# A convolution in two channel passes, merged with a gated layer by a planner that writes the order of every instruction

## The chip, the cores and the metric

The kernel runs on one core of a Trainium2 chip. The metric is the device time of one execution in microseconds; the figure for the kernel before is the median of three runs. Engines are named as the profile names them: PE (TensorE), DVE (VectorE), ACT (ScalarE), POOL (GpSimd), SP (SyncE, which here issues all DMAs).

## What is computed

The input x (2048 positions, 512 channels) goes through two layers, mixed by a gate per position. All is fp32.

```
g  = sigmoid((x * gate_w).sum(-1))
dt = exp(log_dt);  logdA = dt * (A_re + i A_im)                    # 512 x 128
K[d, l] = Re sum_n  C[d,n] * exp(logdA[d,n] * l) * dt * B[d,n]      # l = 0..2047
a  = causal_convolution(x, K, along positions) + x * Dskip          # by FFT in the reference
h  = sigmoid(x @ w_gate) * (x @ w_up)                               # 512 -> 1792
b  = h @ w_down                                                     # 1792 -> 512
out = g * a + (1 - g) * b
```

## The kernel before, in words

**The gated layer** (`glu`, `weights`, `hidden`, L303 to L352 and L373 to L412). Positions are cut into two halves, each into two blocks `sb` of 512. The 1792 hidden columns are 14 tiles `f` of 128, in groups of 4, 4, 3 and 3. Each fp32 operand is split into a high part, rounded to fp32r, and the rest, and a product is three fp32r matmuls (high x high, low x high, high x low). `hidden` makes one tile of h with 24 matmuls (L401), ACT's sigmoid (L408), DVE's product (L409), and the split of h (L410, L411). After each group the down product takes 3 matmuls a tile for each of four blocks of 128 positions (L339), and the result goes to `acc`, by ACT for the first group (L343), by DVE after that (L345). That makes 1344 + 672 matmuls. Weights are loaded and split twice: the first half stores the low part in DRAM (`wlo`), the second loads the raw weights again, rounds them again, and reads the low part back.

**K** (`bases`, `double`, `kgen`, L147 to L241). The 512 channels are 16 groups of 32, with the 128 states n on the partitions. l is written as a sum of two indices, so the exponential is a product of two tables of complex powers, T[:, 0] with 32 entries and T[:, 1:3] with 64. Each is built by doubling: a table of e entries times one power gives the next e, three DVE operations a step (L187, L188, L189: product with the imaginary part, product with the real part, sum). Both tables are doubled together up to 32, and one more step of 128 x 2048 elements makes 64. PE sums over n with 64 products of 32 x 64 a group (L220, `kps`); ACT evicts (L223), DVE adds Dskip, PE applies the first transform step to K (L232), ACT evicts to `kev` (L236), and each two of these tiles of four groups go to DRAM (`a_k`).

**The convolution.** `rows` (L354) takes 16 blocks of x, makes the gate, transforms (L367, two products that use 64 rows of the array each) and stores to `a_u`. When all K is there, `finish` (L252) goes through 16 steps q over all 512 channels: the second step of the transform for x and K (L248, 128 rows by 64 columns, two column halves side by side), the complex product on DVE (L268 to L275), three copies on ACT (L276 to L278) that stack real and imaginary parts in 128 rows, the inverse step (L281), and a store to `b_s`. `final` (L287) reads `b_s` back for each block of 128 positions, applies the last step (L293) and adds g times it to `acc` (L296).

**What sets the order.** The body is written as Python generators. `run_b` lets the gated layer go on by a number of matmuls (`ROW`, `MID`, `END`, `LAST`, L44) at fixed points of the other work. The layer that records the program then sets the order in which the instructions of each engine stand; the last part of `kgen` has high priority. Each engine works through its own stream in order. All DMAs are issued by SP.

Of the kernel before, what the change touches and what calls it, by code (L numbers as in the profile page):

```python
# [13 lines left out]

# [6 lines left out]
F32 = mybir.dt.float32  # L22
# [7 lines left out]
P = 128  # L30
# [4 lines left out]
NG = 16  # L35
KS = [6, 0, 7, 1, 8, 2, 9, 3, 10, 4, 5]
NB = len(KS)
# [3 lines left out]
NQ = 4  # L41

UNITS = 2 * 12 * NF * 6
ROW, MID, END, LAST = 32, 50, 0.7, 0.14  # L44


def constants():
# [5 lines left out]
    wk = np.zeros((4, 32, 2, 4, 32))  # L53
    wf = np.zeros((2, 2, 32, 2, 32))
    for j in range(2):
        for c in range(2):
            for jp in range(2):
                wu[jp, j, :, jp, c, j, :] = fwd[c]
            wf[j, c, :, j, :] = fwd[c].T / L
    for j in range(4):  # L60
        for c in range(2):
            wk[j, :, c, j, :] = fwd[c]
# [3 lines left out]
    for k in range(32):  # L66
# [6 lines left out]
    wv = wv.reshape(16, 2, P, P).transpose(0, 2, 1, 3)  # L73
    e2 = 2.0 ** np.array(KS)
    f = lambda x, *s: np.ascontiguousarray(x.astype(np.float32).reshape(s))
    return {
        "c_wu": f(wu, P, 2, P), "c_wf": f(wf, P, 64), "c_wk": f(wk, P, 2, P),
        "c_pw": f(np.stack([e2, e2 / (2 * np.pi) * np.where(np.array(KS) < 6, -1, 1)]), 1, 2 * NB),
        "c_w2": f(w2, 16, P, 2 * P), "c_wv": f(wv, 16, P, 2 * P),
# [3 lines left out]
def body(ctx, tc, xp, xt, prm, ldt, dsk, gw, wgu, wdn, c_wu, c_wf, c_wk, c_w2, c_wv, c_pw, out):  # L83
    nc = tc.nc
    mm = nc.tensor.matmul
    pool = lambda name, bufs=1, space=None: tc.tile_pool(name=name, bufs=bufs, **({"space": space} if space else {}))

    dr = ctx.enter_context(pool("dr", 1, DRAM))
    a_u = dr.tile([2, 64, 32, D], F32, name="a_u")
    a_k = dr.tile([NQ, P, 32, P], F32, name="a_k")  # L90
    b_s = dr.tile([P, 32, D], F32, name="b_s")
    dts = dr.tile([16, 32], F32, name="dts")
    wlo = dr.tile([NF, P, 1536], F32, name="wlo")
# [3 lines left out]
    bp = ctx.enter_context(pool("bp"))  # L97
    ps = ctx.enter_context(pool("ps", 1, PSUM))

    def fps(tag="fft", bufs=2):  # L100
        return ps.tile([P, 512], F32, tag=tag, bufs=bufs, name="fps")


    wu = cst.tile([P, 2, P], F32, name="wu")
    wk = cst.tile([P, 2, P], F32, name="wk")
    pw = cst.tile([P, 2, NB], F32, name="pw")
    gwb = cst.tile([P, D], F32, name="gwb")
# [5 lines left out]
    nc.vector.memset(hpi, math.pi / 2)  # L113


    def steps():
        st = bp.tile([16, 10, 32], F32, tag="sg", bufs=2, name="steps")
        x, nf, r, e, h1, h2 = (st[:, i] for i in range(6))
        n, pn, b1, b2 = (st[:, i].bitcast(I32) for i in range(6, 10))
        nc.sync.dma_start(x, ldt)  # L120
        V = nc.vector
        V.tensor_scalar(x, x, -104.0, 89.0, op0=OP.max, op1=OP.min)
        V.tensor_scalar(n, x, 1 / math.log(2), None, op0=OP.mult)
        V.tensor_copy(nf, n)
        V.scalar_tensor_tensor(r, nf, -LN2H, x, op0=OP.mult, op1=OP.add)
        V.scalar_tensor_tensor(r, nf, -LN2L, r, op0=OP.mult, op1=OP.add)
        V.tensor_scalar(e, r, 1 / 5040, 1 / 720, op0=OP.mult, op1=OP.add)
        V.tensor_tensor(e, e, r, op=OP.mult)
        for k in (120, 24, 6, 2, 1):
            V.scalar_tensor_tensor(e, e, 1.0 / k, r, op0=OP.add, op1=OP.mult)  # L130
        V.tensor_scalar(e, e, 1.0, None, op0=OP.add)

        for s in (0.5, 1.0):
            V.tensor_scalar(pn, nf, s, None, op0=OP.mult)
            h, b = (h1, b1) if s < 1 else (h2, b2)
            V.tensor_copy(h, pn)
            if s == 1.0:
                V.tensor_tensor(h, h, h1, op=OP.subtract)
# [5 lines left out]
    def tmp(pp):  # L144
        return pp.tile([P, 2048], F32, tag="tmp", bufs=2, name="tmp")
# [359 lines left out]
```

## Time and profile before

| | |
|---|---|
| median of 3 runs | 755.97 us (750.52 to 758.19) |
| the profiled execution: time | 753.36 us |
| the profiled execution: span from the first to the last instruction | 751.6 us |
| mean granted TensorE clock | 0.975 |
| moved by DMA | 118.64 MB, mean 158 GB/s |
| the chain that ended last: PE, DVE, ACT, DMA | 53%, 28%, 8%, 7% |

The page gives busy time of each engine, the span in 40 slices (a digit is a tenth of busy time), the chain of work that ended last, and the costliest groups of instructions by line with count, busy time and mean time of one. PE is the matmuls and PEld the loading of their weights. Matmuls are pipelined, so that a busy PE need not be a PE at its peak: what a matmul costs is read from the time between two starts. A window row gives the busy time of each engine in a stretch of the span.

### The profile page before, as it was taken

To read this page: it belongs to the slowest core of one execution; us is meant where nothing else is said; L and a number is where in the kernel's file an instruction comes from. 1 tells how busy PE (TensorE), PEld (TensorE's weight loads), DVE (VectorE), ACT (ScalarE), POOL (GpSimd) and SP (SyncE) were. 2 spreads that over 40 slices of the span, in tenths; PEclk is the share of its full clock that TensorE was granted. 3 is DMA by queue.
4 is the path that set the end of the run, shared out by engine and by line. 5 is a ranking of instruction groups with operands and counts; after the bars stand their busy time and mean duration, and the time that the engine had idled before them with its cause. 6 is when DMAs were issued, how large, how long until landed. Compare 5 with 4: busy or idle time off the path is not lost.

```text
span 751.6 us, 12658 instructions
## 1 busy us (share of the span) xinstructions
PE 706.8 (94%) x5024; PEld 475.2 (63%) x5024; DVE 604.9 (80%) x835; ACT 375.5 (50%) x611; POOL 3.7 (0%) x36
## 2 busy tenths in 40 slices
PE   4988889998999999999999999999999999999995
PEld 3445348877888778877787787887883323333651
DVE  5888989999999999899999898999944544454343
ACT  5364645763638274655565654546134555555200
POOL 0000000000000000000000000000000000000000
PEclk9789879999999999999999999999999999999999
DMA  6768662433025033565013350531158877774587
GB/s 221 213 204 229 170 178 97 156 104 148 32 88 183 22 115 130 194 237 175 26 57 126 100 189 8 168 115 56 57 187 284 258 241 243 225 223 147 174 285 254
DMA packets 61019, 118.64 MB, mean 158 GB/s; under 512 B 8224, under 2 KB 22944, under 8 KB 59936
## 3 DMA queue, kind: packets, MB, share of 16 engines
q1 hardware_dynamic: 60960, 117.84, 48.3%
q8 instruction: 39, 0.64, 0.3%
q14 instruction: 20, 0.16, 0.1%
HBM read 75.35 MB, written 42.47 MB: 157 GB/s over the span
## 4 chain that ended last, share of the span: by engine, by line
PE 53%; DVE 28%; ACT 8%; DMA 7%; issue 3%; SPq 0%; DVEq 0%; ACTq 0%
PE gups L401 19%; PE dps L339 12%; PE fps L248 9%; DVE T L189 6%; DVE T L188 6%; DVE tmp L187 6%; PE ips L281 4%; PE fps L367 3%; DVE h L409 2%; PE kps L220 2%; DVE hl L411 2%; DMA xs<-xt 2%; PE fps L232 2%; DMA wst<-wgu 1%; PE fps L293 1%
## 5 line engine op out<-in xcount | busy, mean ns | idle before, releaser
L401 PE MATMUL gups<-xh,gu 128*128 128x512 f32 x896 | 293.9, 402 | 15.2 <-ACT gu L381 12.5
L401 PEld LDWEIGHTS gups<-xh,gu 128*128 128x128 f32 x896 | 170.0, 191 | 71.4 <-issue 16.2
L401 PE MATMUL gups<-xl,gu 128*128 128x512 f32 x448 | 179.2, 400 | 0.0
L339 PE MATMUL dps<-dnw,hh 128*128 128x512 f32 x448 | 150.2, 402 | 3.6 <-ACT hh L410 3.0
L187 DVE TENSOR_TENSOR tmp<-T,bz 128x64 f32<-128x64 f32 (+2 forms) x96 | 114.8, 1195 | 2.3 <-issue 0.2
L189 DVE TENSOR_TENSOR T<-T,tmp 128x64 f32<-128x64 f32 (+2 forms) x96 | 114.6, 1194 | 0.7
L188 DVE TENSOR_TENSOR T<-T,bz 128x64 f32<-128x64 f32 (+2 forms) x96 | 114.6, 1193 | 0.0
L339 PEld LDWEIGHTS dps<-dnw,hh 128*128 128x128 f32 x448 | 83.5, 189 | 37.5 <-issue 11.6
L401 PEld LDWEIGHTS gups<-xl,gu 128*128 128x128 f32 x448 | 85.6, 191 | 27.4 <-issue 10.3
L339 PE MATMUL dps<-dnw,hl 128*128 128x512 f32 x224 | 89.6, 401 | 3.0 <-DVE hl L411 1.7
L408 ACT ACTIVATE sg<-gups 128x512 f32<-128x512 f32 x56 | 33.5, 598 | 70.3 <-PE gups L401 69.6
L268 DVE TENSOR_TENSOR t<-fps,uf 128x512 f32<-128x512 f32 x32 | 22.0, 688 | 57.6 <-PE fps L248 47.6
L410 ACT ACTIVATE hh<-h 128x512 fp32r<-128x512 f32 x56 | 35.1, 628 | 47.9 <-DVE h L409 47.9
L409 DVE TENSOR_TENSOR h<-gups,sg 128x512 f32<-128x512 f32 x56 | 38.1, 684 | 20.4 <-PE gups L401 20.1
L339 PEld LDWEIGHTS dps<-dnw,hl 128*128 128x128 f32 x224 | 42.3, 189 | 16.5 <-DVE hl L411 3.7
L411 DVE TENSOR_TENSOR hl<-h,hh 128x512 fp32r<-128x512 f32 x56 | 38.3, 686 | 8.9 <-ACT hh L410 8.4
L381 ACT ACTIVATE gu<-wst 128x1024 fp32r<-128x1024 f32 x28 | 29.6, 1057 | 29.4 <-PE gups L401 13.8
L345 DVE SCALAR_TENSOR_TENSOR acc<-dps,omg,acc 128x512 f32<-128x512 f32 x48 | 35.5, 746 | 10.3 <-PE dps L339 10.3
L248 PE MATMUL fps<-au,w_in 128*64 128x512 f32 x128 | 42.3, 611 | 0.3 <-DVE t L268 0.3
L236 ACT ACTIVATE kev<-fps 128x256 f32<-128x256 f32 x64 | 33.8, 678 | 16.3 <-PE fps L232 15.4
L248 PE MATMUL fps<-ak,w_in 128*64 128x512 f32 x128 | 41.2, 609 | 0.0
L367 PE MATMUL fps<-u,wu 64*128 64x512 f32 x64 | 32.4, 780 | 6.6 <-DMA u<-xp 2.9
(78 smaller groups left out, 664.5 us busy)
## 6 DMA issues: line engine op xcount, KB each, us to landing
wst<-wgu SPq DMA_DIRECT2D x28, 512.0 KB, 4.5
a_u<-evu SPq DMA_DIRECT2D x32, 256.0 KB, 3.3
a_k<-kev SPq DMA_DIRECT2D x8, 1024.0 KB, 6.0
au<-a_u SPq DMA_DIRECT2D x16, 512.0 KB, 4.8
ak<-a_k SPq DMA_DIRECT2D x16, 512.0 KB, 4.2
b_s<-evb SPq DMA_DIRECT2D x32, 256.0 KB, 2.5
b_in<-b_s SPq DMA_DIRECT2D x16, 512.0 KB, 4.6
wsd<-wdn SPq DMA_DIRECT2D x28, 256.0 KB, 3.5
```

The lines of the kernel that those rows point to most:

```text
L187: nc.vector.tensor_tensor(t2, src, sb, op=OP.mult)
L188: nc.vector.tensor_tensor(dst, src, br, op=OP.mult)
L189: nc.vector.tensor_tensor(dst, dst, t2[:, :, ::-1], op=OP.add)
L236: nc.scalar.activation(kv[i][:, s:s + 4], p4[:, :, :, 16 * i:16 * i + 16], AF.Copy)
L248: mm(p[64 * kb:64 * kb + 64], w[:, kb, 64 * c:64 * c + 64], a(kb), start=True, stop=True, tile_position=(0, 64 * kb), skip_group_check=True)
L339: mm(p, a[:, hs], dnw[:, b], start=(n == 0), stop=(n == last))
L345: nc.vector.scalar_tensor_tensor(accs[t], p, omg[:, t:t + 1], accs[t], op0=OP.mult, op1=OP.add)
L367: mm(ph[jp], wu[r, jp], u[r], start=True, stop=True, tile_position=(64 * jp, 0))
L401: mm(p, gu[:, a, k, dc], b[:, dc], start=(n == 0), stop=(n == 11))
L409: nc.vector.tensor_tensor(h, pp[1], sg, op=OP.mult)
L410: nc.scalar.activation(hh, h, AF.Copy)
L411: nc.vector.tensor_tensor(hl, h, hh.bitcast(F32), op=OP.subtract)
```

## The change

The program computes the same, with these differences.

- **The order.** Every piece of work is a generator (a strand) that yields `(engine, cost, function, what it waits for)`. `Plan.run` keeps a clock for each engine, takes the strand whose next piece could start first (its start plus a bias per strand), calls the function, which records the instructions, and books the cost. Costs are constants in the code: `dve(n)` and `act(n)` for n elements, 0.227 a matmul, 1.28 for a change of activation table. `manual_schedule` makes the recorded order the final one. Buffers are single slots, handed out by the planner.
- **K.** The second factor (64 entries) isn't doubled any more. 38 angles per channel and state are formed (`ANGLES`: 0 to 32 and five powers of two), reduced by rounding, and ACT takes sine and cosine of all (L332, L333). ACT also makes 64 magnitudes per channel, with 32 ACTIVATEs of 64 elements a group, each with the scale taken from SBUF (L338). DVE multiplies the two to `B` (L389 to L393), the lower 32 entries with conjugate angles. Only the first factor T (32 entries) is doubled, in five steps (L359 to L361).
- **Packed products.** The first step on K (L434), the inverse step (L582) and the last step (L627) use 64 rows of the array, with the two row halves side by side, and accumulate real and imaginary parts; the three copies that stacked them are gone.
- **Two passes.** The convolution runs over 256 channels at a time (`WIDTHS`). A pass begins when its eight groups of K are stored (`kdone`), so the first pass stands between groups 9 and 12 of K. `a_k` and `b_s` are one DRAM tensor a pass, and a transfer of K to DRAM (L450) has runs of 64 elements.
- **Weights.** The first half stores both parts of the split weights (`wsp`), and the second reads both back; nothing is split twice. Loads and splits go in pieces of 128 x 512.

The gated layer's product is written back to PSUM and split from there. The number of its matmuls, 2016, is the same.

On PE, in the middle of K (the gated layer is L401 and L339 before, L749 and L798 now; kps is the sum over states). Before:

```order
L401 MATMUL gups<-xl,gu 128x512
L220 MATMUL kps<-T 32x64 x64
L339 MATMUL dps<-dnw,hh 128x512
L339 MATMUL dps<-dnw,hl 128x512
L339 MATMUL dps<-dnw,hh 128x512 x2
L339 MATMUL dps<-dnw,hl 128x512
L232 MATMUL fps<-wk,kst 64x128 x16
```

Now, around group 9:

```order
L409 MATMUL kps<-B,T 32x64 x64
L798 MATMUL dps<-dnw,h 128x512 x3
L513 MATMUL s2u<-au,ww 64x256 x4
L749 MATMUL gups<-x,gu 128x512 x6
L513 MATMUL s2u<-au,ww 64x256 x4
L749 MATMUL gups<-x,gu 128x512 x6
L513 MATMUL s2k<-ak,ww 64x256 x4
L798 MATMUL dps<-dnw,h 128x512 x3
L434 MATMUL wps<-wk,kst 64x64 x32
L513 MATMUL s2k<-ak,ww 64x256 x4
L749 MATMUL gups<-x,gu 128x512 x6
L582 MATMUL ips<-y,ww 128x256 x4
```

The first pass of the convolution (L513, L582) has moved between the groups of K, in blocks of four products between three or six matmuls of the gated layer; before, all of it stood behind the last group.

On ACT, the bases of one group (L163 to L172 before, L310 to L346 now; L408/L764 is the sigmoid, L410/L770 the split of h). Before:

```order
L165 ACT_TABLE_LOAD
L165 ACTIVATE tmp<-tmp 128x352
L410 ACTIVATE hh<-h 128x512
L166 ACTIVATE tmp<-tmp 128x352
L167 ACT_TABLE_LOAD
L167 ACTIVATE tmp<-tmp 128x352
L408 ACT_TABLE_LOAD
L408 ACTIVATE sg<-gups 128x512
L382 ACTIVATE dnw<-wsd 128x512
L168 ACT_TABLE_LOAD
L168 ACTIVATE tmp<-tmp,hpi 128x352
L408 ACT_TABLE_LOAD
```

Now:

```order
L331 ACTIVATE mg<-ex 128x1216
L332 ACT_TABLE_LOAD
L332 ACTIVATE ex<-mg,hpi 128x32x38
L770 ACTIVATE h<-gups 128x512
L333 ACTIVATE ex<-ex 128x32x38
L334 ACT_TABLE_LOAD
L334 ACTIVATE e_2473<-e_2473 128x160
L338 ACTIVATE mg<-pw,aa 128x64 x32
L764 ACT_TABLE_LOAD
L764 ACTIVATE sg<-gups 128x512
L346 ACTIVATE bz<-bz 128x160
L770 ACTIVATE h<-gups 128x512
```

The exponentials have become one block of 32 between two table loads, and no sigmoid stands inside it.

On DVE, where the fields of one group are made (B is the second factor, T the first; `mg` are the magnitudes):

```order
L344 TENSOR_TENSOR bz<-ex,e_2834 128x2x160
L376 TENSOR_TENSOR w<-w 128x32
L377 TENSOR_TENSOR w<-w 128x32
L378 TENSOR_TENSOR w<-w,ex 128x64
L379 TENSOR_TENSOR w<-w,ex 128x64
L380 TENSOR_TENSOR T<-w 128x32
L381 TENSOR_TENSOR T<-w 128x32
L425 TENSOR_TENSOR kst<-kst,dskt 128x8
L766 TENSOR_TENSOR gups<-gups,sg 128x512
L389 TENSOR_TENSOR B<-ex,mg 128x64x32
L771 TENSOR_TENSOR h<-gups,h 128x512
L392 TENSOR_TENSOR B<-mg,ex 128x32x32
```

Before, no row of the kind of B existed, and this place held the doubling steps of 128 x 2048 (L187 to L189). A step of the gated layer (L766, which takes a sigmoid `sg`) now stands ahead of B.

The core of the diff:

```diff
+ANGLES = list(range(33)) + [64 << k for k in range(5)]
+NA = len(ANGLES)
+WIDTHS = [256, 256]
...
+    def cost(self, eng, n):
+        if eng == "PE":
+            mode, n = n
+            return n + (0.1 if mode != self.last else 0.0)
+        if eng == "ACT" and isinstance(n, tuple):
+            return n[1] + (1.28 if n[0] != self.kind else 0.0)
+        return n
...
+                    key = start + st[0]
+                    if best is None or key < best[0]:
+                        best = (key, st, eng, m, start)
...
+    ctx.enter_context(tc.manual_schedule())
+    dve = lambda n: 0.067 + n * 1.042e-3
+    act = lambda n: 0.06 + n * 0.88e-3
...
-    def bases(pp, gi):
-        nc.vector.tensor_tensor(th, aa[:, :, None, :].to_broadcast(sh), pw[:, :, :, None].to_broadcast(sh), op=OP.mult)
...
+                V.tensor_tensor(f, aa[:, 1, :, None].to_broadcast([P, 32, NA]), pw[:, None, :NA].to_broadcast([P, 32, NA]), op=OP.mult)
+            t = yield "ACT", act(32 * NA), lambda: A.activation(n, f, AF.Copy), [t, mgs.t]
+            t = yield "DVE", dve(32 * NA), lambda: V.tensor_tensor(f, f, n, op=OP.subtract), [t]
...
+            t = yield "ACT", act(32 * NA), lambda: A.activation(af, f, AF.Abs), [t]
+            t = yield "ACT", ("sin", act(32 * NA)), lambda: A.activation(cs, af, AF.Sin, scale=-2 * math.pi, bias=hpi), [t]
+            t = yield "ACT", ("sin", act(32 * NA)), lambda: A.activation(f, f, AF.Sin, scale=-2 * math.pi), [t]
+            te = yield "ACT", ("exp", act(160)), lambda: A.activation(e5, e5, AF.Exp), [te]
+            def mags():
+                for d in range(32):
+                    A.activation(mg[:, d], pw[:, NA + 5:], AF.Exp, scale=aa[:, 0, d:d + 1])
+            tm = yield "ACT", ("exp", 32 * act(64)), mags, [t]
...
-            double(pp, T[:, 2], T[:, 1], bz, 10, 32, 32)
...
+            yield "DVE", dve(2048), lambda: V.tensor_tensor(
+                B[:, :, :, 32:], ex[:, :, :, :32], mg[:, :, None, 32:].to_broadcast(sh), op=OP.mult), [tb]
+            lo = ex[:, :, :, 32:0:-1]
+            yield "DVE", dve(1024), lambda: V.tensor_tensor(B[:, :, 0, :32], mg[:, :, :32], lo[:, :, 0], op=OP.mult), [tb]
+            tb = yield "DVE", dve(1024) + 0.1, lambda: V.scalar_tensor_tensor(
+                B[:, :, 1, :32], mg[:, :, :32], -1.0, lo[:, :, 1], op0=OP.mult, op1=OP.mult), [tb]
+            for k in range(5):
+                e = 1 << k
+                t = yield from double(T[:, :, :, e:2 * e], T[:, :, :, 0:e], bz[:, :, k], 32, e, t)
...
+            for s in range(8):
+                for jh in range(2):
+                    r = slice(64 * jh, 64 * jh + 64)
+                    for c in range(2):
+                        mm(ph[jh][64 * c:64 * c + 64, 64 * s:64 * s + 64], kst[r, s], wk[r, c], start=True, stop=True,
+                           tile_position=(64 * jh, 64 * c), skip_group_check=True)
...
+            te = yield "SP", kb(1024), lambda: S.dma_start(a_k[j][:, :, o:o + 64], kev), [te]
...
-            nc.scalar.activation(y[:64, 1], y[64:, 0], AF.Copy)
-            nc.scalar.activation(y[64:, 1], t2[64:, 0], AF.Copy)
-            nc.scalar.activation(y[64:, 0], t2[:64, 0], AF.Copy)
-                mm(p, wv[:, kb], y[:, kb], start=True, stop=True)
+            for c in range(2):
+                for i in range(2):
+                    r = slice(64 * i, 64 * i + 64)
+                    mm(pi[i], ww[r, 2 + c], y[r, c], start=(c == 0), stop=(c == 1), tile_position=(64 * i, 0))
...
+            for x in range(4):
+                for jb in range(2):
+                    r = slice(64 * jb, 64 * jb + 64)
+                    mm(ph[jb][32 * x:32 * x + 32], wf[r], b[x // 2][r, x % 2], start=True, stop=True,
+                       tile_position=(64 * jb, 32 * x), skip_group_check=True)
...
+        t1 = yield "SP", kb(1024), lambda: S.dma_start(ga, gf), [t]
+        t2 = yield "SP", kb(512), lambda: S.dma_start(da, df), [t]
+        wstored[f].set(max(t1, t2))
...
+                      (load_x(), 0.0), (load_w(), 0.0), (const("wu", wu, c_wu, kb(128)), 0.2),
+                      (const("gwb", gwb, gw.to_broadcast([P, D]), kb(256)), 0.2), (bases(), 0.2), (tables(), 0.5),
+                      (rows(), 0.0), (const("wk", wk, c_wk, kb(64)), 0.3),
+                      (const("dsk", dskt, dsk.rearrange("p (g s) -> p g s", g=NG), kb(64)), 0.3),
+                      (const("wf", wf, c_wf, kb(16)), 0.4), (hidden(), 1.0), (down(), 0.7), (passes(), 0.1)):
```

898 lines of the change are left out of this document (584 added, 314 removed).

## The prediction

> **What bounds the kernel now.** I read the page's busy line and its 40 slices first, then the table of windows, cut where the last group of K is finished.
>
> ```profile
> PE 706.8 (94%) x5024; PEld 475.2 (63%) x5024; DVE 604.9 (80%) x835; ACT 375.5 (50%) x611; POOL 3.7 (0%) x36
> PE   4988889998999999999999999999999999999995
> DVE  5888989999999999899999898999944544454343
> PEclk9789879999999999999999999999999999999999
> 0.00:20.00 20.00, 9.51 (x28) 6.31 (x28) 11.80 (x44) 10.93 (x16) 0.42 (x6) 1.00 0.70 231
> 20.00:115.00 95.00, 80.89 (x514) 45.36 (x516) 84.27 (x132) 45.91 (x99) 0.43 (x4) 0.82 0.68 194
> 20.00:540.00 520.00, 495.19 (x4156) 380.82 (x4157) 494.18 (x645) 281.86 (x459) 3.24 (x30) 0.97 0.40 128
> 540.00:751.00 211.00, 202.06 (x842) 88.05 (x840) 98.89 (x148) 82.74 (x137) 0.00 (x0) 0.99 0.68 225
> ```
>
> In the window rows the numbers behind the length are busy us (and instructions) of PE, PEld, DVE, ACT and POOL, then granted clock, DMA share and GB/s. There are two kernels in one. Until 540 us VectorE is the limit: 494.18 of 520 us. PE shows 495.19 there too, but a busy PE is not a full one. Behind 540 VectorE is half idle and PE is at its limit (202.06 of 211). To see what PE's work is worth I take prices from unbroken runs in the chain and the PE timeline, at a granted clock of 1.00:
>
> ```profile
> 433.17 16.80 PE gups L401 x74
> 427.32 1.93 PE kps L220 x128
> 430.61 1.90 PE fps L232 x32
> 655.34 1.08 PE L248 MATMUL fps<-au,w_in 128*64 128x512 f32 x4
> 656.25 1.95 PE L248 MATMUL fps<-ak,w_in 128*64 128x512 f32 x8
> 658.13 0.50 PE L339 MATMUL dps<-dnw,hh 128*128 128x512 f32 x1
> 658.47 1.08 PE L281 MATMUL ips<-y,wv 128*128 128x512 f32 x2
> 659.48 1.07 PE L248 MATMUL fps<-au,w_in 128*64 128x512 f32 x2
> ```
>
> A matmul of the gated part is 16.80/74 = 0.227 us. An fp32 product counts as two instructions; start to start, a pair of 64-column products over 512 columns (x4) takes 0.91 us, two pairs (x8) 1.88, a full-width product (L281, x2) 1.01. With these prices the tail holds 842 - 384 = 458 gated matmuls (104 us) and the 384 conv instructions (64 pairs of L248, 32 products of L281 and 16 pairs of L293, at 1.0: 112 us): 216, against 211 measured, so the prices hold within 3%. The K part holds the other 1558 gated matmuls (354 us) and 16 groups of K and rows (some 85 us): 439 us of PE work in 540. So PE has 100 us to spare while VectorE builds K, and nothing to spare afterwards.
>
> **The change part by part.** *PE.* The gated matmuls stay: 2016 x 0.227 = 457.6. L409 is 64 products a group as L220 was: 16 x 1.93 = 30.9. L434 has half the columns in four 64x64 tiles; kps ran 128 instructions of 64 columns in 1.93 us on four tiles, so 64 take 1.0: 16.0 (before 30.4). L513 does per channel half what L248 did: 64 blocks of 1.0 = 64. L582 replaces a full-width product by two 64-row halves side by side, 32 blocks, and L627 a pair by eight 64x32 tiles, 16 blocks. Whether row halves overlap is read from the only row-split product of before:
>
> ```profile
> 103.60 1.33 PE L367 MATMUL fps<-u,wu 64*128 64x512 f32 x4
> 103.60:104.90 1.30, 1.30 (x4) 0.50 (x4) 0.83 0.85 292
> 77.45 1.54 PE L367 MATMUL fps<-u,wu 64*128 64x512 f32 x4
> ```
>
> Four instructions one after another, at the quarter of 0.91 x 2 that one costs alone (0.46), would be 1.8 us; they took 1.33, at a clock of 0.83 besides. So they overlap, at least in part: the bounds of such a block are 0.9 (as column pairs) and 1.8 (not at all). I take 1.0 for L582 and L627, nearer to the column pairs, and 1.3 for L484: 32 + 16 + 20.8. Sum 637.3 us; by the same prices before is 655. PE's work hardly shrinks. What moves is the place: half of the convolution now stands between the groups of K, in the 100 us that were to spare. Counted in the new order, 488.5 us of PE stand ahead of the last kps (1620 gated matmuls, 15 groups, all rows, one pass and its finals) and 148.8 from it on; 87.0 of the first stand ahead of the second kps.
>
> *VectorE.* Rows by form:
>
> ```profile
> L187 DVE TENSOR_TENSOR tmp<-T,bz 128x2048 f32<-128x2048 f32 x32 | 73.1, 2285 | 0.2
> L187 DVE TENSOR_TENSOR tmp<-T,bz 128x1024 f32<-128x1024 f32 x16 | 19.5, 1221 | 0.3
> L187 DVE TENSOR_TENSOR tmp<-T,bz 128x512 f32<-128x512 f32 x16 | 11.0, 690 | 0.3
> L187 DVE TENSOR_TENSOR tmp<-T,bz 128x256 f32<-128x256 f32 x16 | 6.8, 424 | 0.4 <-issue 0.2
> L187 DVE TENSOR_TENSOR tmp<-T,bz 128x64 f32<-128x64 f32 x16 | 4.3, 269 | 1.1
> L171 DVE TENSOR_TENSOR bz<-tmp 128x704 f32<-128x704 f32 x16 | 14.2, 885 | 0.1
> ```
>
> Doubling falls from 3 x (0.27 + 0.42 + 0.69 + 1.22 + 2 x 2.29) = 21.5 us a group to 3 x (0.27 + 0.34 + 0.42 + 0.69 + 1.22) = 8.8. Added: B (2.29 + 1.22 + 1.25 = 4.8), two passes over 1216 angles (1.42 each, between the rows of 1024 and 2048), e5, bz and small ones; the bases' old products go. With the bases and the start a group falls from 25.2 to 19.7, x 16 = -88 us. Smaller pieces elsewhere cost +10 (64 combines of 256 at 0.42 for 32 of 512, weights in three pieces, 32 finals). So 605 becomes about 527, some 445 ahead of the last B. VectorE stops being the one limit, but it is still 445 us in a stretch where PE has 488.
>
> *ScalarE* pays for it.
>
> ```profile
> L204 ACT ACTIVATE T<-bz 128x64 f32<-128x64 f32 x16 | 5.0, 315 | 0.0
> L343 ACT ACTIVATE acc<-dps,omg 128x512 f32<-128x512 f32 x16 | 10.8, 684 | 15.8 <-PE dps L339 15.6
> L223 ACT ACTIVATE kst<-kps 128x512 f32<-128x512 f32 x16 | 9.5, 597 | 12.7 <-PE kps L220 12.5
> 20.20 0.30 ACT L204 ACTIVATE T<-bz 128x64 f32<-128x64 f32 x1
> 20.35 0.19 ACT L361 ACTIVATE g<-gl 128x1 f32<-128x1 f32 x1
> L408 ACT ACT_TABLE_LOAD x22 | 28.2, 1283 | 0.7 <-PE gups L401 0.4
> L166 ACT ACTIVATE tmp<-tmp 128x352 f32<-128x352 f32 x16 | 7.8, 485 | 1.1 <-DVE tmp L164 1.1
> ```
>
> L338 is 512 exponentials of 64 elements, 32 in a row, each with its scale read from memory. The nearest row of that size holds the engine 20.35 - 20.20 = 0.15 us; a scale from memory adds 684 - 597 = 0.09 (L343 against L223). Bounds 0.15 and 0.24; I take 0.235, which L343's surcharge speaks for: 7.5 us a group, 120 in all. The planner's own table charges 0.06 + 64 x 0.00088 = 0.116, or 3.7 us a group: its order was made for a shorter ScalarE. Four ACTIVATEs of 1216 a group replace four of 352 (+2.4 a group), table loads go from 59 to 70 (+14), three y copies (-30) and the second split of the weights (-21) go: 375 becomes some 490-500.
>
> *The cycle of one group.* ex, mg, bz and T have one buffer each, so groups follow in a ring: angles 1.6, n 1.1, subtract 1.4, abs 1.1, load and two sines 3.6, load and e5 1.5, 32 exponentials 7.5, B 4.8: 22.6 us, with hand-overs 24. In the order the next sigmoid (load 1.3) and its two VectorE steps stand ahead of B in most groups: 27.5. Engine work per group is of the same size: 445/16 = 27.8 on VectorE, 401.5/14 = 28.7 on PE. No engine has slack to hide the others' lateness.
>
> *DMA.* wsp writes and reads both halves, two passes read c_ww twice: about 15 MB more on 118.64, no limit. L450 writes K in runs of 256 bytes, 4096 a transfer:
>
> ```profile
> a_k<-kev SPq DMA_DIRECT2D x8, 1024.0 KB, 6.0
> q1 hardware_dynamic: 60960, 117.84, 48.3%
> ```
>
> A packet took on average 0.483 x 16 x 751.6 / 60960 = 95 ns of an engine at 1.9 KB; 256 packets an engine lie between the 6 us of the old write and 24 us. Each pass waits for the last of four: 0 to 36 us in all. I put none in the sum, because the pieces are an eighth of the mean, and keep the 36 for the range. The Trainium skill, "DMA: Bandwidth & Descriptors", section "Specifications", speaks against it: full rate only from 512 bytes, below that a read-modify-write. By that a transfer might take twice its 6 us, 12 more over the two passes; no run here shows it yet.
>
> **The sum.** First gated matmul at about 13 us: its third weight piece is the fifteenth DMA, and these rows show 0.46 us between issues, with a landing of about 3.5:
>
> ```profile
> 1.19 0.41 SPq L427 DMA_DIRECT2D pw<-c_pw  x1
> 1.65 0.42 SPq L150 DMA_DIRECT2D pg<-prm  x1
> xs<-xt SPq DMA_DIRECT2D x16, 256.0 KB, 3.5
> 736.07 4.04 DMA out<-o
> ```
>
> The first 87 us of PE work lose 15%, as PE idled 14 of 95 us in 20:115 (rows, x and weights all wait for DMA): 100. The rest of the K part loses VectorE's idle share plus PE's, 5.0% + 4.2%, because each is now near its limit and waits for the other: 401.5 x 1.09 = 437.6. The tail loses 4.5%: 155.5. Last add and store 4.5 (0.4 and the store's 4.04). Span 711; plus 1.8 outside it (753.36 against 751.6): **712 us**. The profiled run stood 2.6 under the median of 755.97, inside the spread of the three runs.
>
> **The rivals.** (1) *PE's sum holds nearly bare:* the order is good enough that only 3% is lost: 13 + 656 + 4.5 + 1.8 = 676; with L484, L582 and L627 at 0.9 it is 664. For it: VectorE already ran at 95% over 520 us. Against: three engines are full at once, and ScalarE is dearer than planned. (2) *The ring of K takes over, slower than before:* in-order engines make each of some eleven hand-overs wait for what stands ahead. With 36 us of VectorE work ahead of the first B and 10 us of doubling and kps behind the last, the K part ends as in the sum at 33.6 us a cycle (36 + 15 x 33.6 + 10 = 550); from 36 us on, 586 plus 155.5 + 4.5 + 1.8 = 748, it decides; at 38 us the time is 778. For it: 27.5 us with no waiting at all and sigmoid loads between. Against: VectorE's 15 to 19 us of doubling and splits run beside the exponentials. (3) *Row halves don't overlap:* L582, L627 and L434 at 1.8 add 26 + 13 + 13: 764 if all sits on PE, some 750 where PE waits anyway. The 1.33 us row speaks against it. (4) *The 256-byte writes hold up each pass* by 12 to 18 us: 742.
>
> **How the numbers follow.** A difference of 1% (7.6 us) is about what can be told from no change. Chances: the sum 0.56 (own range 685 to 742), rival 1 0.16, rival 2 0.12, rival 3 0.07, rival 4 0.09. Range 665 to 762: it takes in rivals 1, 3 and 4 and the sum, and leaves rival 2's far part and the lowest of rival 1. Faster by over 1% (under 748.4): 0.53 of the sum's, 0.16, 0.08 of rival 4's and 0.04 of rival 3's, together 0.81; within 1%: 0.02 + 0.01 + 0.03 = 0.06; slower: rival 2 and 0.01 of the sum's, 0.13.
>
> **What would show it.** Right: VectorE busy near 527 and ScalarE near 490; L338 spaced 0.21 to 0.24; L582 blocks near 1.0; the last kps at 535 to 550 us; PE idle share of 8 to 10% until then, named by ScalarE or VectorE. Wrong: PE idle under 4% (rival 1), a steady group spacing of 36 or more with ScalarE at the end of PE's waits (rival 2), L582 blocks at 1.8 (rival 3), s2k waiting for ak after the last L450 (rival 4).

## The result, and the profile after

The changed kernel takes **823.59 us** (median of four runs, 823.27 to 825.69), the kernel before 753.63 (four runs, 750.52 to 758.19): ratio 1.093, 95% interval 1.086 to 1.100. It is 9% slower. The forecast of 712 and its range up to 762 missed.

The busy line, three rows of the slices (the last the granted clock) and the chain's shares by engine, from the page of the changed kernel:

```profile
PE 708.2 (86%) x6176; PEld 503.8 (61%) x6176; DVE 537.1 (65%) x1011; ACT 496.6 (60%) x1102; POOL 0.2 (0%) x4
...
PE   3869887888889988978898879897997989999997
...
DVE  6658386887878876976586848666896444353332
ACT  4958939788587793677776867693966222222000
...
PEclk9879898999999997998899999899999999999998
...
PE 39%; ACT 33%; DMA 14%; DVE 7%; issue 3%; SPq 3%; DVEq 0%; ACTq 0%
```

VectorE and ScalarE are as busy as forecast (537 for 527, 497 for 490 to 500). But no engine is full now: from 60 us to 640 PE's slices swing between 7 and 9, and ScalarE, 60% busy, holds a third of the chain that ended last.

The K products of all groups, one row: durations, then first and last start.

```profile
L409 PE MATMUL kps<-B,T x2048: 216/219/314, 81.2 to 645.7; 128*32 128x64 f32 x187
```

The last kps starts at 645.7, where 535 to 550 was forecast; a group takes (645.7 - 81.2)/15 = 37.6 us. The windows, cut at the first, second and last kps (columns as in the prediction):

```profile
0.00:81.00 81.00, 57.15 (x195) 36.71 (x195) 55.72 (x123) 55.94 (x111) 0.20 (x4) 0.89 0.70 231
81.00:133.00 52.00, 45.34 (x354) 29.72 (x356) 33.99 (x66) 38.24 (x95) 0.00 (x0) 0.90 0.50 144
133.00:646.00 513.00, 447.87 (x4670) 333.35 (x4663) 382.10 (x704) 367.39 (x823) 0.00 (x0) 0.95 0.47 152
646.00:821.00 175.00, 157.84 (x972) 104.02 (x972) 65.31 (x119) 35.04 (x75) 0.00 (x0) 0.99 0.54 171
```

Set against the terms of the sum (us; the stages are the prediction's):

| stage | PE as priced | length forecast | PE busy | PE idle | length measured |
|---|---|---|---|---|---|
| to the second kps | 87.0 | 113 | 102.5 | 30.5 | 133 |
| to the last kps | 401.5 | 437.6 | 447.9 | 65.1 | 513 |
| behind it | 148.8 | 160 | 157.8 | 17.9 | 175.7 |
| sum | 637.3 | 711 | 708.2 | 113.5 | 821.7 |

Of the 111 us that the forecast lacks, 71 are PE busy time above its price, and 40 are more idle time than the 74 allowed. (The first term was short too: the first gated matmul starts at 18.0 us, where 13 was forecast.) The waits (engine and line, what was waited for, total us, how often, the longest) say where the idle time is:

```profile
ACT h L770 <- DVE gups L766: 65.9, 33, 6.8
...
DVE gups L766 <- PE gups L749: 43.5, 24, 5.0
...
PE dps L798 <- ACT h L770: 28.9, 13, 6.9
...
DVE gups L766 <- ACT sg L764: 23.9, 13, 8.6
```

PE waits for h, and h for VectorE's product. That product waits 43.5 us for PE's own matmuls and 23.9 us for the sigmoid. The chain of one group shows what stands ahead of the sigmoid (start, length, what):

```profile
264.38 1.28 ACT L334
265.67 0.34 ACT e L334
266.01 7.67 ACT mg L338 x32
273.70 1.28 ACT L764
274.99 0.61 ACT sg L764
275.62 0.71 DVE gups L766
276.36 0.61 ACT h L770
276.99 0.69 DVE h L771
...
278.76 2.28 DVE B L389
281.05 1.14 DVE B L392
282.19 1.13 DVE B L393
...
284.19 1.44 DVE ex L315
...
285.71 1.23 ACT mg L317
```

The 32 exponentials hold ScalarE for 7.67 us; the sigmoid's table load and the sigmoid wait for that; VectorE's queue has the sigmoid's product and the split of h ahead of B; only behind B are ex and mg free for the next group's angles. So in this group the ring of K (the steps that use ex and mg from one group's angles to the next group's) and the gated layer stop each other by turns, and everything in these rows is on the chain.

### The profile page after: what moved, and what is told of

Same layout as the page of the kernel before. It is cut to its first block, busy times and chain, and to the rows that moved or that the text cites. A ratio compares the mean times of both kernels' runs of the same rounds, so it can differ in the third digit from the quotient of the medians.

```text
span 821.7 us, 15690 instructions
## 1 busy us (share of the span) xinstructions
PE 708.2 (86%) x6176; PEld 503.8 (61%) x6176; DVE 537.1 (65%) x1011; ACT 496.6 (60%) x1102; POOL 0.2 (0%) x4
## 4 chain that ended last, share of the span: by engine, by line
PE 39%; ACT 33%; DMA 14%; DVE 7%; issue 3%; SPq 3%; DVEq 0%; ACTq 0%
PE gups L749 18%; ACT mg L338 14%; PE dps L798 8%; DMA au<-a_u 6%; PE ips L582 4%; PE s2u L513 2%; PE s2k L513 2%; ACT L334 2%; PE wps L434 2%; ACT L764 2%; PE ups L484 2%; ACT ex L332 2%; DMA al<-acc 2%; ACT mg L331 2%; ACT L332 2%
## 5 line engine op out<-in xcount | busy, mean ns | idle before, releaser
L749 PE MATMUL gups<-x,gu 128*128 128x512 f32 x1344 | 341.7, 407 | 10.4 <-DMA gu<-wsp 5.3
L749 PEld LDWEIGHTS gups<-x,gu 128*128 128x128 f32 x1344 | 257.8, 195 | 86.0 <-issue 17.8
L798 PE MATMUL dps<-dnw,h 128*128 128x512 f32 x672 | 187.9, 420 | 36.3 <-ACT h L770 28.9
L798 PEld LDWEIGHTS dps<-dnw,h 128*128 128x128 f32 x672 | 127.5, 198 | 89.5 <-ACT h L770 35.6
L338 ACT ACTIVATE mg<-pw,aa 128x64 f32<-128x64 f32 x512 | 124.1, 335 | 0.0
L766 DVE TENSOR_TENSOR gups<-gups,sg 128x512 f32<-128x512 f32 x56 | 39.1, 698 | 67.7 <-PE gups L749 43.5
L770 ACT ACTIVATE h<-gups 128x512 fp32r<-128x512 f32 x56 | 33.3, 594 | 65.9 <-DVE gups L766 65.9
L771 DVE TENSOR_TENSOR h<-gups,h 128x512 fp32r<-128x512 f32 x56 | 38.5, 688 | 27.9 <-ACT h L770 27.2
L764 ACT ACTIVATE sg<-gups 128x512 f32<-128x512 f32 x56 | 33.5, 598 | 34.0 <-PE gups L749 33.6
L361 DVE TENSOR_TENSOR T<-T,t 128x64 f32<-128x64 f32 (+4 forms) x80 | 46.5, 581 | 1.8
L359 DVE TENSOR_TENSOR t<-T,bz 128x64 f32<-128x64 f32 (+4 forms) x80 | 46.2, 577 | 1.6
L513 PE MATMUL s2u<-au,ww 128*64 128x256 f32 x256 | 34.7, 390 | 14.3 <-DMA au<-a_u 13.8
L360 DVE TENSOR_TENSOR T<-T,bz 128x64 f32<-128x64 f32 (+4 forms) x80 | 46.0, 575 | 0.0
L582 PE MATMUL ips<-y,ww 64*128 64x256 f32 x256 | 37.7, 410 | 3.6 <-ACT ev L589 3.4
L409 PE MATMUL kps<-B,T 128*32 128x64 f32 x2048 | 33.6, 226 | 7.1 <-DVE T L361 5.8
```

What stands on the lines that cost most here:

```text
L338: A.activation(mg[:, d], pw[:, NA + 5:], AF.Exp, scale=aa[:, 0, d:d + 1])
L359: yield "DVE", dve(n), lambda: V.tensor_tensor(t2, src, sb, op=OP.mult), [t, slot.t]
L360: t = yield "DVE", dve(n), lambda: V.tensor_tensor(dst, src, br, op=OP.mult), [t]
L361: t = yield "DVE", dve(n), lambda: V.tensor_tensor(dst, dst, t2[:, :, ::-1], op=OP.add), [t]
L409: mm(p[32 * jj:32 * jj + 32, s], T[:, ch, c], B[:, ch, c], start=(c == 0), stop=(c == 1), tile_position=(0, 32 * jj), skip_group_check=True)
L513: mm(p[64 * kb_:64 * kb_ + 64, c], ww[:, kb_, 64 * c:64 * c + 64], a(kb_), start=True, stop=True, tile_position=(0, 64 * kb_), skip_group_ ...
```

## The experiments

The theories, as they arose: **1** the ring of K, with 7.7 us of exponentials in it, sets the cycle. **2** The written order is at fault, not one length in it. **3** The tail is late since loads stand behind stores in SyncE's queue. **4** PE is the limit all along, its work dearer than priced. **5** and **6** split theory 2: the unbroken run of 32 exponentials, or the weights (bias constants) by which the planner chooses. "Free order" means without the line `tc.manual_schedule()`: the recording layer then orders each engine's instructions, as it does in the kernel before. All times are medians; the kernel before stood at 754 to 758 beside them.

| run | us | first, last kps | a group | tail | PE busy | clock |
|---|---|---|---|---|---|---|
| the change | 823.6 | 81.2, 645.7 | 37.6 | 176 | 708.2 | 0.949 |
| exp1 | 765.1 | 74.0, 591.2 | 34.5 | 174 | 691.3 | 0.975 |
| oneexp | 782.0 | 77.2, 603.6 | 35.1 | 176 | 692.0 | 0.971 |
| price | 823.0 | 87.1, 667.4 | 38.7 | 152 | 707.9 | 0.938 |
| auto | 758.7 | 77.7, 589.7 | 34.1 | 169 | 701.1 | 0.986 |
| fixpe | 812.7 | 76.7, 644.2 | 37.8 | 168 | 639.7 | 0.907 |
| autope | 741.5 | 77.4, 581.5 | 33.6 | 160 | 643.5 | 0.930 |
| autoone | 744.8 | 76.2, 572.2 | 33.1 | 169 | 700.5 | 0.991 |
| autoonepe | 700.6 | 75.2, 540.2 | 31.0 | 158 | 620.9 | 0.962 |
| latepass | 816.4 | 76.3, 548.4 | 31.5 | 266 | 717.4 | 0.931 |
| poolq | 815.7 | 81.1, 650.8 | 38.0 | 167 | 708.1 | 0.943 |
| chunk8 | 868.6 | 100.5, 715.7 | 41.0 | 148 | 713.2 | 0.919 |
| pricebias | 794.6 | 84.8, 636.4 | 36.8 | 160 | 700.6 | 0.955 |
| best | 748.6 | 72.3, 591.3 | 34.6 | 155 | 679.3 | 0.984 |
| autobest | 732.4 | 66.7, 577.8 | 34.1 | 152 | 684.7 | 0.982 |

"A group" is (last - first)/15; the tail is the span minus the last kps; the clock is the granted one. From the last kps on there are 396 matmuls of the gated layer in the change, exp1, oneexp, autoone and poolq, 386 in auto, 348 in pricebias, 324 in best and autobest, 234 in price, 144 in latepass and none in chunk8; "a group" and the tail can be compared only where these are alike. fixpe's profile is of its longest run.

### Shorter exponentials in the same order: exp1 and oneexp

```
 exp1:
-for d in range(32):
-    A.activation(mg[:, d], pw[:, NA + 5:], AF.Exp, scale=aa[:, 0, d:d + 1])
+A.activation(mg, pw[:, None, NA + 5:].to_broadcast([P, 32, 64]), AF.Exp, scale=-0.02)
 oneexp, in place of the same two lines:
+sm = [P, 32, 64]
+V.tensor_tensor(mg, aa[:, 0, :, None].to_broadcast(sm), pw[:, None, NA + 5:].to_broadcast(sm), op=OP.mult)
+A.activation(mg, mg, AF.Exp)
```

> The 32 exponentials of a group (L338) become one instruction over 2048 elements with one constant scale; every instruction keeps its place in the order. It leaves out each channel's own decay rate, so the output is not the reference's. ScalarE should hold the group's magnitudes for about 1.9 us (0.06 + 2048 x 0.88 ns, worked out from the 1216-element rows) in place of 7.75, so a group's ring gets 5.8 us shorter. Theory 1 (the ring of K through ScalarE's exponentials sets the cycle): the cycle falls from 37.5 to about 32-33, last kps at 555-580 instead of 646, time 735-765. Theory 2 (the fixed order, not any one length in it, makes the engines wait for each other): last kps stays above 620, time 795-820. Theory 3 (the other half of the miss, the tail, has its own cause in the queue of loads): whatever happens to the K part, the stretch from the last kps to the end stays at 170-180 us.

> The same places in the order, the result kept: one VectorE product of 128x2048 (index times each channel's rate) and one ScalarE exponential of 2048 in place of the 32. The ring loses 7.75 us and gains 2.3 + 1.9: net 3.5 us a group, and VectorE gains 16 x 2.3 = 37 us of work. Theory 1: 823 - 16 x 3.5 = 767 (750-785), cycle about 34. Theory 2: 800-825. A third reading, that VectorE's own work would set the cycle: above 823.

exp1 gives 765.05, oneexp 782.03. A group falls by 3.1 and 2.5 us, where the ring got 5.9 and 3.5 shorter. So the exponentials stand in what sets the cycle, and the length of one step, with no instruction moved, is worth 58.5 us. But exp1 kept only half of its gain a group, and its last kps (591) came later than theory 1 said (555 to 580). From the starts of the instructions (mean of groups 2 to 16): the time from the last exponential to B grew from 5.3 to 8.0 us, with the exponentials done; VectorE is at other work for 5.5 of these 8.0 us. Theory 2's 795 to 820 is out, and theory 3's statement that the tail stays (174, 176) holds.

### The order: price and auto

```
 price:
-            tm = yield "ACT", ("exp", 32 * act(64)), mags, [t]
+            tm = yield "ACT", ("exp", 32 * 0.242), mags, [t]
 auto:
-    ctx.enter_context(tc.manual_schedule())
```

> Only the planner's price of the 32 exponentials is put right, from 3.7 to 7.74 us a group, and the order is made anew; no instruction gets shorter. Theory 1 (the length itself): 800-830, the ring is as long as before. Theory 2 (the order was made for a shorter ScalarE, and the work behind each exponential stands in the wrong place): 750-780, with PE's waits for ScalarE gone and last kps before 590.

> The written-out order is handed to the recording layer, which may place each engine's instructions by its own rules. Theory 2 (a rigid order): 760-800. Theory 1: no order takes the exponentials out of the ring, 810-850.

price gives 822.98: in total, the planner's too low price is not what costs the time, as theory 1 said. auto gives 758.72, and against theory 1: with every instruction of the change, the 32 exponentials at their full length, the free order takes 65 us less (ratio to the kernel before 1.004, interval 1.000 to 1.008). The busy line, PE's row of the slices and three groups of auto:

```profile
PE 701.1 (92%) x6176; PEld 488.3 (64%) x6176; DVE 523.5 (69%) x1011; ACT 544.7 (72%) x1142; POOL 0.2 (0%) x4
...
PE   4779999979999999999999989999999989999997
```

```profile
L337 ACT ACTIVATE mg<-pw,aa 128x64 f32<-128x64 f32 x512 | 131.3, 338 | 7.6 <-DVE aa L303 6.3 <-DVE aa L313 0.9
L337 ACT ACT_TABLE_LOAD x39 | 50.0, 1283 | 3.9 <-DVE aa L303 1.8 <-DVE B L392 1.5
L763 ACT ACT_TABLE_LOAD x34 | 43.6, 1283 | 1.5 <-PE gups L748 0.9
```

ScalarE does 48 us more here, which 40 more table loads (51 us) account for, and the kernel is faster than the change. The timeline of ScalarE in auto shows what it bought (start, length, line, operation, instructions in a row):

```profile
301.81 0.35 ACT L337 ACTIVATE mg<-pw,aa 128x64 f32<-128x64 f32 x1
302.18 1.28 ACT L763 ACT_TABLE_LOAD   x1
303.48 0.60 ACT L763 ACTIVATE sg<-gups 128x512 f32<-128x512 f32 x1
304.09 1.28 ACT L337 ACT_TABLE_LOAD   x1
305.39 1.79 ACT L337 ACTIVATE mg<-pw,aa 128x64 f32<-128x64 f32 x7
307.07 1.22 ACT L316 ACTIVATE mg<-ex 128x1216 int32<-128x1216 f32 x1
308.19 1.30 ACT L337 ACTIVATE mg<-pw,aa 128x64 f32<-128x64 f32 x5
309.78 1.22 ACT L330 ACTIVATE mg<-ex 128x1216 f32<-128x1216 f32 x1 [0.29 <-DVE ex L317]
```

In this group thirteen of the 32 exponentials run beside the angles, ahead of the absolute value (they write the part of mg in which the angles do not lie), and a sigmoid breaks in between. So it is in 5 of the 16 groups; in the others 1 to 9 run early, 121 of 512 in all. In the changed kernel all 32 stand behind the sines, as a block. The wait of dps for h falls from 28.9 to 6.4 us.

### Less work for PE: fixpe and autope

```
-for n, (a, b) in enumerate(((0, 0), (0, 1), (1, 0))):
-    mm(p, gu[:, a, k, dc], x[:, b, dc], start=(dc + n == 0), stop=(dc == NC - 1 and n == 2))
+for n, (a, b) in enumerate(((0, 0), (0, 1))):
+    mm(p, gu[:, a, k, dc], x[:, b, dc], start=(dc + n == 0), stop=(dc == NC - 1 and n == 1))
```

> The changed kernel in its own order, with the third product of each hidden matmul (low part of the weights) left out: 448 of 6176 PE instructions, 448 x 0.227 = 102 us of PE work, 83 of it ahead of the last kps and 19 behind it. Leaves out a correction term of the hidden layer's products. Theory 1 and 2 (ScalarE in the ring, or the written order, hold PE up, PE itself is not the limit ahead of the last kps): only the 19 us of the tail come off in full, 790-805. Theory 4 (PE is the limit all along): 720-745.

> The same 448 matmuls left out, with the order left to the recording layer (758.7 us with them). Leaves out the same correction term. Theory 4 (with a free order PE is the limit, at 701 us busy of 758, and so it was in the kernel before, at 707 of 752): 655-690. Theory 1 (the ring of K still sets the cycle, 34.1 us): 735-745, since only the 19 us behind the last kps come off.

With 102 us of PE work gone by price, the changed kernel loses 11 us (812.73, 8 above what theories 1 and 2 gave; its four runs spread from 802.1 to 814.1) and the free order 17 (741.46). PE's busy time falls by less than the price, by 69 and 58 us: the granted clock is lower, and a matmul of dps takes 436 and 420 ns where it took 420 and 407. Even so a PE that sets the time would have given back 58 us and not 17. The last kps hardly moves: 645.7 to 644.2, and 589.7 to 581.5. So PE is not what sets the K part, with either order: theory 4 falls for these two, and theory 1 gets its number in autope (735 to 745). In the waits of fixpe PE only waits longer for the same thing:

```profile
PE dps L798 <- ACT h L770: 47.5, 18, 10.2
```

### Both: autoone, autoonepe, best and autobest

autoone is auto with oneexp's edit, autoonepe takes the third product out of it as well. best is a written order again, made with the true prices and other weights; autobest is the same with a free order:

```
 best:
+            tm = yield "DVE", dve(2048), lambda: V.tensor_tensor(
+                mg, aa[:, 0, :, None].to_broadcast(sm), pw[:, None, NA + 5:].to_broadcast(sm), op=OP.mult), [t]
+            tm = yield "ACT", ("exp", act(2048)), lambda: A.activation(mg, mg, AF.Exp), [tm]
...
-(bases(), 0.2), (tables(), 0.5), ... (hidden(), 1.0), (down(), 0.7)
+(bases(), 0.2), (tables(), 0.3), ... (hidden(), 0.7), (down(), 0.7)
 autobest, besides:
-    ctx.enter_context(tc.manual_schedule())
```

> The order left to the recording layer, and the 32 exponentials replaced by one product on VectorE and one exponential of 2048, result kept. Theory 4 (PE is the limit): 748-762, next to nothing beside 758.7. Theory 1 (ring of K): 16 x 3.5 = 56 us off, 700-715. Something between would say that ScalarE's 545 us still hold PE up in places.

> The written order, made anew for the one exponential of 2048 and its VectorE product with their true prices, and with other bias constants for K (0.3 in place of 0.5) and the hidden layer (0.7 in place of 1.0); result kept. Theory 2 (a written order that is made with true prices loses little): 740-762, PE busy 92% as with the free order. Theory 1: as the same edit in the old order, 775-790.

> Free order, one exponential of 2048, and the third product of each hidden matmul left out (448 matmuls, 102 us of PE work; a correction term of the hidden layer is missing). Theory 4 (with ScalarE relieved, PE is the limit at 700 us busy of 742): most of the 102 us comes off, 655-690. Theory 1 (a ring of K of 33 us sets the cycle even so): only the tail's 19 us, 720-735.

> Free order, one exponential of 2048 with its true price, and the planner's bias constants 0.3 for K's tables and 0.7 for the hidden layer. Theory 4 (PE limit at some 700 us busy and 35-40 us of unavoidable start, end and waits): 735-748. Below 730 would say that the order still held PE up in the run without the new constants.

autoone 744.76: 14 us come off. That is 3 us below theory 4's 748 to 762 and far from theory 1's 700 to 715. Where PE is 94% busy, a shorter ring buys little. autoonepe 700.64: 44 of the 102 us come off, between the two theories, so with the exponentials out of the way PE is a part of the limit and not all of it; VectorE is at 9 in most slices of the K part there. best 748.63, within what was expected of a written order with true prices and other weights. autobest 732.39 is the fastest, faster than the kernel before too (ratio 0.966, interval 0.963 to 0.970), some 3 us below its expected range. From its page:

```profile
PE 684.7 (94%) x6176; PEld 485.8 (67%) x6176; DVE 553.3 (76%) x1029; ACT 432.6 (59%) x625; POOL 0.2 (0%) x4
```

PE busy plus 45 us of start, end and waits is the span, 730.1.

### The first pass held back: latepass

```
 (on autoone)
-            yield kdone[j]
+            yield kdone[-1]
```

> Free order, one exponential of 2048, and the first channel pass held back until all of K is stored, so that no convolution step stands between the groups of K any more: some 62 us of PE work (16 steps of 3.2 us and 10 us of finals) move behind the last kps. Theory 4 (PE is full ahead of the last kps, so what leaves that stretch shortens it): the last kps comes 45-62 us earlier, at 510-527, and the time stays at 740-765. Theory of the prediction (PE has some 100 us to spare while K is built): the last kps stays at 560-575 and the time grows by about 60, to 795-810.

816.38, 72 us slower than autoone, and above what both theories gave. The last kps comes at 548, 24 us earlier. What moved is more than the pass. These are the gated matmuls from the last kps on, first L749 and L798 of autoone, then the same of latepass (the first number in a bracket is the count):

```profile
572.20:741.50 169.30, 64.61 (x252) 45.90 (x252) 1.00 0.54 167
572.20:741.50 169.30, 39.55 (x144) 25.54 (x144) 1.00 0.54 167
548.40:814.20 265.80, 20.62 (x78) 14.02 (x78) 0.79 0.60 179
548.40:814.20 265.80, 17.04 (x66) 11.92 (x66) 0.79 0.60 179
```

While the pass was held back, the gated layer went on in its place: 252 of its matmuls, 57 us at 0.227, moved ahead of the last kps. By the prediction's prices PE's work behind the last kps is then the same, 148.8 us in autoone and 147.6 in latepass. So the run does not measure how much room PE had while K is built, and neither theory is tested by it. What it shows is the tail, which takes 97 us more (266 against 169) for the same priced work:

```profile
548.00:813.00 265.00, 199.51 (x1276) 104.94 (x1264) 88.26 (x177) 47.48 (x108) 0.00 (x0) 0.80 0.61 180
```

With 144 gated matmuls beside 32 steps, in place of 396 beside 16, the gaps between the steps stay open, and the granted clock falls to 0.80. In this program the merged pass is therefore worth 72 us, measured without the written order. That is no measure against the kernel before: it keeps 270 gated matmuls (162 of L401, 108 of L339) for its tail and takes 204 us from the last kps to the end, with the whole convolution in it.

### The loads of the tail: poolq

```
-ta = yield "SP", kb(w), lambda: S.dma_start(au, src), ...
+ta = yield "SP", kb(w), lambda: nc.gpsimd.dma_start(au, src), ...
 (and so for ak, b_in and al)
```

> The changed kernel in its written order, with the loads of the passes and of the finals (au, ak, b_in, al) issued by GpSimd in place of SyncE, so that they no longer stand behind stores in one queue. Theory 3 (the tail is late because loads stand behind stores in SyncE's queue): the stretch from the last kps to the end falls from 176 to 160-168, time 805-815. Otherwise (the tail is PE's work, dearer than priced): 174-180 and 820-826; slower if loads issued there take longer to land.

815.69: the tail falls from 176 to 167, theory 3's number, and its reason holds in part. These rows of the changed kernel stand in the chain of the tail, and the wait below them is SyncE's longest there:

```profile
668.81 1.11 PE ips L582 x8
...
669.94 0.33 SPq L534
...
670.31 5.55 DMA au<-a_u
...
772.41 0.54 SPq L644
...
773.48 2.37 DMA al<-acc
```

```profile
SPq L534 <- PE ips L582: 55.6, 13, 8.4
```

The loads of al stand behind stores of the output (L644), as theory 3 says. What stands ahead of the load of au is no store but the load of the next weights ww (L534), which waits until the inverse product has freed their buffer. Behind the last kps au held 10% of the chain and al 6%; in poolq au is not among its named shares and al is at 2%. So the 9 us of the tail are loads that SyncE issued late. They come off although each load now costs GpSimd time (88 us busy in all).

### What in the written order: chunk8 and pricebias

```
 chunk8:
-            tm = yield "ACT", ("exp", 32 * act(64)), mags, [t]
+            for d0 in range(0, 32, 8):
+                def mags(d0=d0): ...            # d0 to d0 + 8
+                tm = yield "ACT", ("exp", 8 * 0.242), mags, [t]
 pricebias, besides price's edit:
-(bases(), 0.2), (tables(), 0.5), ... (hidden(), 1.0)
+(bases(), 0.1), (tables(), 0.3), ... (hidden(), 0.7)
```

> Written order, made anew with the true price, the 32 exponentials of a group handed to the planner as four pieces of 8, so that a sigmoid can stand between them. Theory 5 (the unbroken run of 32 on ScalarE is what holds the sigmoids, and PE behind them): 760-785, as with the free order. Theory 6 (the weights by which the order is made): no gain, and each break costs two table loads of 1.28 us in the ring of K: 820-860.

> Written order with the true price and the 32 exponentials whole; only the bias constants of K (0.1 and 0.3 in place of 0.2 and 0.5) and of the hidden layer (0.7 in place of 1.0) changed. Theory 5: 810-830, the run is as long as before. Theory 6: 770-795.

chunk8 takes 868.61, more than either theory said: with the run broken into four, and 104 table loads where the change has 70, a group costs 41 us. So theory 5's 760 to 785 did not come. A clean test of theory 5 it is not, since the new order also puts all gated matmuls ahead of the last kps; the 396 that the change keeps behind it are 90 us by price, 6 a group. auto has 110 loads and 34.1 us a group, so the number of loads alone does not decide either. pricebias takes 794.61: other weights alone are worth 28 us of the 65, at the upper edge of theory 6's range. What brings the other 36 (early exponentials, sigmoids let in when they are ready, VectorE's own order, all of which auto changes at once) was not taken apart and stays open.

## Why the prediction was wrong

- **What failed** is the sum's middle term, "401.5 x 1.09 = 437.6", and behind it the step on the cycle of one group. The factor 1.09 was made from two engines' idle shares in the kernel before. The ring was put at 22.6 us of work, 24 with hand-overs and 27.5 with a sigmoid, and so left out of the sum. The stretch took 513 us, and the cycle measures 37.6. By its pieces in the changed kernel (mean of groups 2 to 16, from the starts): angles to the first exponential 15.4 (10.3 forecast), exponentials 7.8 (7.5), then 5.3 until B starts, B 6.4 (4.8), and 3.2 until the next angles: 38.1. These pieces close the cycle whatever sets it; that the exponentials are in what sets it is shown by exp1. Only the prices of the pieces were counted, 22.6 us. In some 11 of the 15 us between them the engine of the next piece is at other work that stands ahead of it, and in the rest it is idle.
- **Rival 2** named this: a spacing of 36 or more with ScalarE at the end of PE's waits, and slower than before. It had 0.12, on the ground that VectorE's doubling runs beside the exponentials. It does, but that does not bring B closer: exp1 shows B waiting for VectorE instead. At 37.6 its formula gives 36 + 15 x 37.6 + 10 + 161.8 = 772. The other 52 us are a first kps at 81, where 36 and 10 were assumed, and a tail of 176 (160).
- **"PE has 100 us to spare while VectorE builds K"** was too high, by a miscount first. "The tail holds 842 - 384 = 458 gated matmuls" takes the last group of K for gated work. These rows of the kernel before are L401, L339, L220 and L232 in the same stretch:

```profile
540.00:751.00 211.00, 52.22 (x186) 33.29 (x186) 0.99 0.68 225
540.00:751.00 211.00, 30.05 (x112) 19.68 (x110) 0.99 0.68 225
540.00:751.00 211.00, 1.99 (x128) 1.83 (x128) 0.99 0.68 225
540.00:751.00 211.00, 1.97 (x32) 1.73 (x32) 0.99 0.68 225
```

  So 298 are gated. By the same prices the tail is 184 us and not 216, 13% short of the 211 measured: the check that "the prices hold within 3%" came out by the miscount. Ahead of it stand 1718 gated matmuls, 471 us of PE work in 540, and 69 to spare. Then the bare price, 655 us for the kernel before, was set beside 706.8 us busy, and the difference called emptiness. In the twelve runs of the table with all of PE's work its busy time is 42 to 80 us above 637 (in the three with 102 less, 621 to 644 against 536). Even autobest, where PE hardly waits, has 47. By that, some 42 of the 111 us that the forecast lacks are PE's price, and not the ring. How much room the merged pass found is not measured.
- **The idle share of PE** in "5.0% + 4.2%" is 4.8% by its row (24.8 of 520 us; 4.2% is that of the row behind it, 8.9 of 211), which would make the middle term 441, 3 us more.
- **The prices of single blocks held**: in the chain of the tail the blocks of L513 stand at 0.86 to 1.08 us and those of L582 at 1.06 to 1.13 (1.0 taken), wps at 1.17 (1.0), kps at 1.92 (1.93). Rival 3 is refuted: the eight row-half instructions of L582 overlap.
- **The exponential** was rightly taken at 0.235: 7.67 us for 32 is 0.24 each, twice the planner's price. The Trainium skill, "ScalarE: Activation LUTs", section "What ACT_TABLE_LOAD costs", gives 186 ns plus 0.833 ns an element, 93 more for an operand read from memory and 93 of overlap; for 64 elements that is an estimate of 0.239 us, and the trace agrees. That "its order was made for a shorter ScalarE" does not matter, though: price (822.98) shows it.
- **The 256-byte writes** were rightly put at none. These rows are of the changed kernel:

```profile
wsp<-gu SPq DMA_DIRECT2D x14, 1024.0 KB, 6.1
...
a_k<-kev SPq DMA_DIRECT2D x8, 1024.0 KB, 6.9
```

  6.9 us to landing for the same megabyte that took 6.0 before: one chain row of 6.81 us, between the last group and the last loads of K, is what rival 4 got in the second pass. The rule of the Trainium skill that the prediction weighed ("DMA: Bandwidth & Descriptors", section "Specifications") says that transfers under 512 bytes miss the full rate, which the prediction read as up to twice the time. The direction agrees, the size here is 15%; the measurement decides.
- **The tail** was to lose 4.5%. It is 16 us longer than forecast: 9 us of PE time above its price and 7 more of idle time. poolq takes back 9.
- **VectorE** fell by 68 us (605 to 537; 78 forecast), and no gain of time shows. In auto, with 81 us less on VectorE and the pass merged, the time is that of the kernel before, within 0.8%.

In sum: this written order costs the change 65 us against a free one, 36 with the weights of pricebias. Without it the other parts bring no measurable gain as they stand, and 26 us (758.1 against 732.4) once one exponential replaces the 32 and the weights are others.

## What to carry to other kernels

- Before a stage is priced by engine sums, close each ring of single buffers: follow one buffer from its first writer to the next, and count at each hand-over what stands ahead in that engine's in-order queue. If the ring comes near the engines' content (27.5 beside 28 us a group here), put it in the sum, not in a rival.
- Set an engine's priced work beside its busy time in the same stage of the profile. Where they differ (by 8% here), expect a difference in the new kernel too; it was 42 to 80 us in the runs of this one.
- Count the instructions of each kind on both sides of a boundary before "842 - 384" is called gated work, and again after an edit that lets the order change: in latepass 57 us of gated work moved one way for the half of the convolution, 56 us by price, that the edit moved the other.
- An order that is written out by hand is a change of its own. Try the same instructions with the order left free before any one of them is blamed.

## What the hardware showed beside that

The granted clock went down where PE's gaps grew, though PE had less to do: with 448 matmuls taken out it fell from 0.949 to between 0.907 and 0.920 (fixpe's four runs) and from 0.986 to 0.930 (autope), and it was 0.80 in latepass's tail, where PE was busy for 199.5 of 265 us. The matmuls that are left get dearer with it: one of dps takes 407 ns in auto (0.986) and 420 in autope (0.930), and the busy time fell by 58 us there where the matmuls taken out were priced at 102. The Trainium skill, "TensorE: Matmul & The Clock Gate", section "A second HAM failure mode: psum-queue depth-cycling", describes, for another kernel, frequent short pauses between groups of matmuls that let the gate swing between half and full rate; the direction agrees with these runs, and how much of the 24 us of busy time between the change (708.2) and autobest (684.7) is the clock was not measured apart.
